# One core, attention and two MoE stages: a weight conversion's ScalarE and VectorE steps put into other slots of its schedule

## The chip, the core and the metric

The kernel runs on one core of a Trainium2 chip. The metric is the device time of one launch in microseconds (us). TensorE (PE, its weight loads apart as PEld), VectorE (DVE), ScalarE (ACT) and GpSimd (POOL) each take their instructions in the order in which the program wrote them; SyncE (SP) issues most loads, GpSimd's queue issues a few. An instruction that waits holds everything behind it on its own engine.

## What is computed

Three stages, all in fp32 accuracy. The second and the third are what matters here; the reference, cut down:

```
x = attention(q, k, v, alpha)                        # 3072 tokens x 384
for e in range(8):                                   # each token goes to one of 8 experts
    mask = argmax(x @ w_gate, axis=1) == e
    h = np.maximum(x[mask] @ w1[e], 0.0)             # 384 -> 1024
    out[mask] = gate_w * sigmoid(x @ w_output_gate)[e] * (h @ w2[e])   # 1024 -> 384
h = (out @ m_w1) * (out @ m_w2) @ m_w3               # the third stage's weights: float64
y = h @ m_w_out
```

The weights of the third stage come as 64-bit words. The kernel turns each word into an fp32 number itself, by integer steps on its two 32-bit halves.

## The kernel before, in words

Every matmul is done as three (`mm3`, lines 155 to 157): each operand is split into a rounded part and a rest, both of which TensorE takes at its fast rate. So every weight piece of 128 x 768 numbers costs ScalarE a copy (`w`, line 146) and VectorE a subtraction of two operands in SBUF (`w`, line 147); `feed` does that, some pieces ahead of their use.

The second stage runs expert by expert, in order of size (464 rows for the first, 360 for the eighth; `e` counts from 0). An expert has an **up** half and a **down** half of eight steps each, `f` = 0 to 7. A step is nine matmuls:

- up step `f`: nine matmuls `u<-xt,w`; then ScalarE writes the rounded `h` (line 822) and VectorE the rest (line 823), both out of the PSUM tile `u`. There are three `u` tiles, so up step `f` can't start before VectorE has done `h` of step `f-3`.
- down step `f`: nine matmuls `d<-h,w`. After `f` = 1, 3, 5 four (or three) transposes turn rows of the next expert, and ScalarE and VectorE write them as `xt` (lines 772, 773). The down half ends with three copies to `yT` on ScalarE (line 835).
- after each odd step there is one `feed`. After `f` = 5 of a down half GpSimd issues the gathers `xg` (line 754) of the expert after next.

Between the last two experts stand the 192 matmuls of `w_prime` (line 935 copies their result).

The conversion is a generator. The loop over experts calls `next(conv, None)` once after each up and each down step from expert 1 on: one such call is a **slot**. Each of the 23 pieces (`N_D`) takes four slots in turn, one piece after the other, and the last slot of each ends with the store of the result to `wm_d` in DRAM over GpSimd's queue (line 856). The stored pieces come back later as `raw` and are fed like the others. In the kernel before, slot 0 of a piece stands behind a step with `f` = 0 or 4. The steps of a piece: `Abs` of the high half into `cva` (ScalarE, line 121; two buffers), the low half scaled into `cvc` (ScalarE, line 122; one buffer), two one-operand steps on `cva` (VectorE, lines 124 and 125), one step with the high half and `cva` (VectorE, line 127), and the addition `cva + cvc` (GpSimd, line 130). `read()` issues the load of the piece after next into the buffer `mraw` that the piece has left (SP, line 852).

Of the kernel before, what the change touches and what calls it, by code (L numbers as in the profile page):

```python
# [11 lines left out]
U32 = mybir.dt.uint32  # L12
ACTF = mybir.ActivationFunctionType
ALU = mybir.AluOpType
# [38 lines left out]
def attention_then_moe_kernel(ctx, tc, pk0, pka, pkb, wbd_d, wexp, wmlp, cst_d, out):  # L53
    nc = tc.nc
    V, A, G, T, SP = nc.vector, nc.scalar, nc.gpsimd, nc.tensor, nc.sync
# [60 lines left out]
    def words(raw, read):  # L116
        w = raw.rearrange("p (n t) -> p n t", t=2)
        lw, hw = w[:, :, 0], w[:, :, 1]
        a, c = [pools["cv"].tile([128, NPC], I32, tag=t, name="cv" + t, bufs=n) for t, n in (("a", 2), ("c", 1))]
        af = a.bitcast(F32)  # L120
        A.activation(out=af, in_=hw.bitcast(F32), func=ACTF.Abs)  # L121
        A.activation(out=c, in_=lw.bitcast(U32), func=ACTF.Copy, scale=2.0 ** -29)
        yield
        V.tensor_scalar(out=af, in0=af, scalar1=TINY, scalar2=None, op0=ALU.max)
        V.tensor_scalar(out=a, in0=a, scalar1=3, scalar2=0x3FFFFFF8, op0=ALU.logical_shift_left, op1=ALU.bitwise_and)
        yield
        V.scalar_tensor_tensor(out=a, in0=hw, scalar=-(1 << 30), in1=a, op0=ALU.bitwise_and, op1=ALU.bitwise_or)
        read()
        yield
        G.tensor_tensor(out=a, in0=a, in1=c, op=ALU.add)  # L130
        return a.bitcast(F32)

# [349 lines left out]
    for j in range(NJ):  # L482
# [22 lines left out]
        if j == 5:  # L505
            A.activation(out=row, in_=cst[:, C_E4:C_E4 + E], func=ACTF.Copy, scale=1024.0)
            V.scalar_tensor_tensor(out=revc, in0=cst[:, C_E4:C_E4 + E], scalar=-1024.0 * E, in1=rev, op0=ALU.mult,
                                   op1=ALU.add)
# [7 lines left out]
        if j in R_RANK:  # L516
# [39 lines left out]
                           op0=ALU.mult, op1=ALU.add)  # L556
# [292 lines left out]
    def m_load(i):  # L849
        if i < N_D:  # L850
            mraw[i] = pools["mr"].tile([128, 2 * NPC], I32, tag="mr", name="mraw")
            SP.dma_start(out=mraw[i], in_=wmlp_w[i])

    def m_convert(i):
        a = yield from words(mraw.pop(i), lambda: m_load(i + 2))
        G.dma_start(out=wm_d[i], in_=a)
        yield
# [94 lines left out]
    def convert_all():  # L952
        m_load(0)
        m_load(1)
        for _ in range(4):
            yield
        for i in range(N_D):
            yield from m_convert(i)

    for e in range(E):  # L960
        if e == 1:
            for _ in conv:
                pass
            lr.close()
            pools["cv"] = cv2.enter_context(tc.tile_pool(name="cvb", bufs=1, reuse_waits="tile"))
            pools["mr"] = cv2.enter_context(tc.tile_pool(name="mr", bufs=2, reuse_waits="tile"))
            conv = convert_all()
# [168 lines left out]
```

## Time and profile before

| | |
|---|---|
| median of 3 runs | 732.04 us (731.51 to 733.71) |
| the profiled execution | 734.38 us, of which the span from first to last instruction is 732.6 |
| TensorE busy | 689.3 us, 94% of the span |
| VectorE, ScalarE, GpSimd busy | 400.3, 338.0, 208.4 us |
| granted TensorE clock | 0.98 over the span |
| stretch in which the pieces are converted, about 190 to 365 us | TensorE busy 173.51 of the 180 us from 185 to 365, VectorE 139.74, ScalarE 111.32, GpSimd 76.04 |

Attention ends at about 143 us. Experts 0 to 6 take 143 to 361 us, `w_prime` 361 to 395, expert 7 395 to 420, and the third stage the rest. Matmuls overlap, so one matmul's duration is longer than the distance to the next start; where the rest of this text speaks of a step's length it takes distances between starts.

### The profile page before, as it was taken

The page shows a single profiled execution, that of the slowest core. Times are in us where ns is not written, and L with a number is a line of the kernel's source. Part 1 is how long each engine was busy: PE and PEld are TensorE (multiplying, and loading weights), DVE is VectorE, ACT ScalarE, POOL GpSimd, SP SyncE. Part 2 cuts the span into 40 slices and gives each one's busy share as a digit, 9 for nine tenths or more (in the row PEclk, how much of TensorE's full clock was granted, in tenths as well). Part 3 has the DMA queues.
Part 4 walks back from the last instruction along what each step waited for, and adds up shares of the span by engine and source line. Part 5 has one row for each costly group of instructions (what it writes and reads, how often), then busy time and mean ns, then how long its engine had stood idle before and what let it go on. Part 6 is the DMA issues. An engine that isn't in the chain of part 4 may idle for free.

```text
span 732.6 us, 14570 instructions
## 1 busy us (share of the span) xinstructions
PE 689.3 (94%) x5856; PEld 610.3 (83%) x5856; DVE 400.3 (55%) x723; ACT 338.0 (46%) x666; POOL 208.4 (28%) x233
## 2 busy tenths in 40 slices
PE   6989998789999999998999999999999999999993
PEld 3877787378999998997999988988889889889893
DVE  6989897678689778687734565033132231340320
ACT  3787786344656756656634554133122222331320
POOL 2977685225153544435310000200101101002001
PEclk7999999899999999999999999999999999999997
DMA  8899883464686887878644500100000000001000
GB/s 275 234 256 252 247 261 109 139 214 162 221 296 234 303 285 262 299 250 297 216 150 152 173 1 0 44 1 12 32 1 22 21 1 34 11 1 44 0 12 33
DMA packets 28200, 101.73 MB, mean 139 GB/s; under 512 B 4784, under 2 KB 5208, under 8 KB 28128
## 3 DMA queue, kind: packets, MB, share of 16 engines
q1 hardware_dynamic: 21360, 77.26, 32.9%
q0 software_dynamic: 6624, 23.29, 9.2%
q8 instruction: 47, 0.77, 0.4%
q14 instruction: 25, 0.20, 0.1%
q10 hardware_dynamic: 144, 0.20, 0.1%
HBM read 82.25 MB, written 18.48 MB: 138 GB/s over the span
## 4 chain that ended last, share of the span: by engine, by line
PE 64%; DVE 4%; issue 4%; POOL 3%; ACT 2%; DMA 2%; POOLq 0%; ACTq 0%
PE pab L157 9%; PE pab L155 9%; PE pab L156 9%; PE o L157 4%; PE o L156 4%; PE o L155 4%; PE d L155 4%; PE u L155 4%; PE d L156 4%; PE d L157 4%; PE u L157 4%; PE u L156 4%; POOL cva L130 3%; DVE w L147 2%; ACT w L146 1%
## 5 line engine op out<-in xcount | busy, mean ns | idle before, releaser
L147 DVE TENSOR_TENSOR w<-raw,w 128x768 fp32r<-128x768 f32 x87 | 103.5, 1193 | 57.6 <-ACT w L146 56.3
L1029 DVE TENSOR_TENSOR p_s<-pab,a_s 128x512 f32<-128x512 f32 x48 | 33.2, 692 | 168.4 <-PE pab L157 168.4
L1043 POOL DMA_INDIRECT out_dram<-o_s,idx_o x24 | 23.4, 974 | 331.6 <-ACT o_s L1042 327.9
L155 PE MATMUL pab<-ys,w 128*128 128x512 f32 x288 | 113.8, 395 | 0.0
L157 PE MATMUL pab<-ys,w 128*128 128x512 f32 x288 | 113.8, 395 | 0.0
L156 PE MATMUL pab<-ys,w 128*128 128x512 f32 x288 | 113.8, 395 | 0.0
L146 ACT ACTIVATE w<-raw 128x768 fp32r<-128x768 f32 x87 | 73.0, 842 | 51.6 <-PE d L157 21.2
L1031 ACT ACTIVATE ab<-p_s 128x512 fp32r<-128x512 f32 x48 | 30.4, 634 | 105.5 <-DVE p_s L1029 105.5
L155 PE MATMUL u<-xt,w 128*128 128x464 f32 (+7 forms) x192 | 69.0, 360 | 8.8 <-DVE h L823 8.1
L130 POOL TENSOR_TENSOR cva<-cva,cvc 128x768 int32<-128x768 int32 x23 | 47.0, 2044 | 95.9 <-ACT cva L121 32.4
L156 PE MATMUL u<-xt,w 128*128 128x464 f32 (+7 forms) x192 | 67.6, 352 | 1.5 <-DVE xt L773 1.5
L155 PE MATMUL d<-h,w 128*128 128x464 f32 (+7 forms) x192 | 68.9, 359 | 0.0
L157 PE MATMUL u<-xt,w 128*128 128x464 f32 (+7 forms) x192 | 67.2, 350 | 0.0
L156 PE MATMUL d<-h,w 128*128 128x464 f32 (+7 forms) x192 | 66.9, 348 | 0.0
L157 PE MATMUL d<-h,w 128*128 128x464 f32 (+7 forms) x192 | 66.6, 347 | 0.0
L157 PEld LDWEIGHTS pab<-ys,w 128*128 128x128 f32 x288 | 54.0, 187 | 13.3
L156 PEld LDWEIGHTS pab<-ys,w 128*128 128x128 f32 x288 | 54.0, 187 | 12.9
L155 PEld LDWEIGHTS pab<-ys,w 128*128 128x128 f32 x288 | 54.0, 187 | 12.9
L155 PE MATMUL o<-wpp,ab 128*128 128x384 f32 x192 | 64.2, 334 | 0.0
L157 PE MATMUL o<-wpp,ab 128*128 128x384 f32 x192 | 64.2, 334 | 0.0
L156 PE MATMUL o<-wpp,ab 128*128 128x384 f32 x192 | 64.2, 334 | 0.0
L1032 DVE TENSOR_TENSOR ab<-p_s,ab 128x512 fp32r<-128x512 f32 x48 | 33.2, 693 | 33.6 <-ACT ab L1031 33.6
(187 smaller groups left out, 1436.1 us busy)
## 6 DMA issues: line engine op xcount, KB each, us to landing
raw<-in_wexp_dram SPq DMA_DIRECT2D x32, 768.0 KB, 5.1
mraw<-in_wmlp_dram SPq DMA_DIRECT2D x23, 768.0 KB, 4.3
pb<-in_pkb_dram SPq DMA_DIRECT2D x24, 384.0 KB, 5.0
wm_d<-cva POOLq DMA_DIRECT2D x23, 384.0 KB, 3.9
raw<-wm_d SPq DMA_DIRECT2D x23, 384.0 KB, 3.7
pa<-in_pka_dram SPq DMA_DIRECT2D x42, 192.0 KB, 4.9
x_d<-xs POOLq DMA_DIRECT2D x23, 192.0 KB, 4.6
pa<-in_pka_dram SPq DMA_DIRECT2D x42, 97.5 KB, 5.1
```

Source lines behind the costliest of these rows:

```text
L130: G.tensor_tensor(out=a, in0=a, in1=c, op=ALU.add)
L146: A.activation(out=hl[:, 0], in_=src, func=ACTF.Copy)
L147: V.tensor_tensor(out=hl[:, 1], in0=src, in1=hl[:, 0], op=ALU.subtract)
L155: T.matmul(out=ps, lhsT=sh, rhs=mh, start=start, stop=False)
L156: T.matmul(out=ps, lhsT=sh, rhs=ml, start=False, stop=False)
L157: T.matmul(out=ps, lhsT=sl, rhs=mh, start=False, stop=stop)
L1029: V.tensor_tensor(out=p_s, in0=pss[1], in1=a_s, op=ALU.mult)
L1031: A.activation(out=t[:, 0], in_=p_s, func=ACTF.Copy)
L1032: V.tensor_tensor(out=t[:, 1], in0=p_s, in1=t[:, 0], op=ALU.subtract)
L1043: G.indirect_dma_start(out=out[:, :], out_offset=bass.IndirectOffsetOnAxis(ap=idx_o[:, n:n + 1], axis=0), in_=o, in_offset=None)
```

## The change

The copy of the low half moves from slot 0 to slot 3, ahead of `read()` and the addition. VectorE's three steps, which stood in slots 1 and 2, stand together in slot 1; slot 2 is empty. The whole sequence starts one slot later, so slot 0 now stands behind `f` = 1 or 5.

```diff
         A.activation(out=af, in_=hw.bitcast(F32), func=ACTF.Abs)
-        A.activation(out=c, in_=lw.bitcast(U32), func=ACTF.Copy, scale=2.0 ** -29)
         yield
         V.tensor_scalar(out=af, in0=af, scalar1=TINY, scalar2=None, op0=ALU.max)
         V.tensor_scalar(out=a, in0=a, scalar1=3, scalar2=0x3FFFFFF8, op0=ALU.logical_shift_left, op1=ALU.bitwise_and)
-        yield
         V.scalar_tensor_tensor(out=a, in0=hw, scalar=-(1 << 30), in1=a, op0=ALU.bitwise_and, op1=ALU.bitwise_or)
+        yield
+        yield
+        A.activation(out=c, in_=lw.bitcast(U32), func=ACTF.Copy, scale=2.0 ** -29)
         read()
-        yield
         G.tensor_tensor(out=a, in0=a, in1=c, op=ALU.add)
...
-        for _ in range(4):
+        for _ in range(5):
             yield
```

ScalarE at the start of expert 6's up half, before (`h` is the rounded half of an up step, in order of `f`):

```order
L822 ACTIVATE h_5132<-u 128x376
L121 ACTIVATE cva<-mraw 128x768
L122 ACTIVATE cvc<-mraw 128x768
L822 ACTIVATE h_5149<-u 128x376
L146 ACTIVATE w_5152<-raw 128x768
L822 ACTIVATE h_5167<-u 128x376
L822 ACTIVATE h_5183<-u 128x376
L146 ACTIVATE w_5186<-raw 128x768
L822 ACTIVATE h_5204<-u 128x376
```

And with the change:

```order
L822 ACTIVATE h_5127<-u 128x376
L128 ACTIVATE cvc<-mraw 128x768
L822 ACTIVATE h_5145<-u 128x376
L146 ACTIVATE w_5148<-raw 128x768
L121 ACTIVATE cva<-mraw 128x768
L822 ACTIVATE h_5164<-u 128x376
L822 ACTIVATE h_5180<-u 128x376
L146 ACTIVATE w_5183<-raw 128x768
L822 ACTIVATE h_5199<-u 128x376
```

The copy `cvc` that now stands behind `h` of step 0 belongs to the piece whose `Abs` ran four slots earlier; the `Abs` of the next piece has moved one step down, behind `w`.

VectorE over the same steps, before:

```order
L823 SCALAR_TENSOR_TENSOR h_5132<-u,h_5132 128x376
L823 SCALAR_TENSOR_TENSOR h_5149<-u,h_5149 128x376
L147 TENSOR_TENSOR w_5152<-raw,w_5152 128x768
L124 TENSOR_SCALAR cva<-cva 128x768
L125 TENSOR_SCALAR cva<-cva 128x768
L823 SCALAR_TENSOR_TENSOR h_5167<-u,h_5167 128x376
L127 SCALAR_TENSOR_TENSOR cva<-mraw,cva 128x768
L823 SCALAR_TENSOR_TENSOR h_5183<-u,h_5183 128x376
L147 TENSOR_TENSOR w_5186<-raw,w_5186 128x768
```

And with the change:

```order
L823 SCALAR_TENSOR_TENSOR h_5127<-u,h_5127 128x376
L823 SCALAR_TENSOR_TENSOR h_5145<-u,h_5145 128x376
L147 TENSOR_TENSOR w_5148<-raw,w_5148 128x768
L823 SCALAR_TENSOR_TENSOR h_5164<-u,h_5164 128x376
L123 TENSOR_SCALAR cva<-cva 128x768
L124 TENSOR_SCALAR cva<-cva 128x768
L125 SCALAR_TENSOR_TENSOR cva<-mraw,cva 128x768
L823 SCALAR_TENSOR_TENSOR h_5180<-u,h_5180 128x376
L147 TENSOR_TENSOR w_5183<-raw,w_5183 128x768
```

`h` of step 2 now stands ahead of all three steps of the conversion instead of between them; `h` of step 3 stands behind all three, as before.

ScalarE at the start of expert 7, behind `w_prime`, one piece of the difference:

```order
+L822 ACTIVATE h0_5660<-u_5650 128x360
+L146 ACTIVATE w1_5663<-raw_5627 128x768
+L128 ACTIVATE cvc_5358<-mraw_5274 128x768
 L822 ACTIVATE h1_5679<-u_5669 128x360
-L146 ACTIVATE w1_5682<-raw_5650 128x768
+L146 ACTIVATE w1_5682<-raw_5627 128x768
 L822 ACTIVATE h2_5698<-u_5688 128x360
```

The last piece's copy, and with it its addition and store on GpSimd, now falls into the first slot of expert 7. GpSimd's own order is the same in both kernels.

## Rows read from the trace of the kernel before

**Rows 1.** TensorE's waits, 200 to 360 us: total, times, longest

```profile
PE u L155 <- DVE h L823: 5.1, 7, 0.9
PE u L156 <- DVE xt L773: 1.3, 1, 1.3
```

**Rows 2.** Timeline of TensorE, expert 6's up half: start, duration, [idle before]

```profile
331.56 0.34 PE L155 MATMUL u<-xt,w 128*128 128x376 f32 x1
...
332.59 0.33 PE L155 MATMUL u<-xt,w 128*128 128x376 f32 x1
334.25 0.44 PE L156 MATMUL u<-xt,w 128*128 128x376 f32 x1 [1.33 <-DVE xt L773]
334.52 0.33 PE L157 MATMUL u<-xt,w 128*128 128x376 f32 x1
...
342.25 0.44 PE L155 MATMUL u<-xt,w 128*128 128x376 f32 x1 [0.86 <-DVE h L823]
...
346.38 0.45 PE L155 MATMUL u<-xt,w 128*128 128x376 f32 x1 [0.78 <-DVE h L823]
...
348.04 0.34 PE L155 MATMUL d<-h,w 128*128 128x376 f32 x1
```

**Rows 3.** Timeline of VectorE in the same half

```profile
339.71 0.96 DVE L147 TENSOR_TENSOR w<-raw,w 128x768 fp32r<-128x768 f32 x1 [0.18 <-ACT w L146]
340.59 0.56 DVE L124 TENSOR_SCALAR cva<-cva 128x768 f32<-128x768 f32 x1
341.18 0.56 DVE L125 TENSOR_SCALAR cva<-cva 128x768 int32<-128x768 int32 x1
...
342.11 0.95 DVE L127 SCALAR_TENSOR_TENSOR cva<-mraw,cva 128x768 int32<-128x768 int32 x1
342.98 0.54 DVE L823 SCALAR_TENSOR_TENSOR h<-u,h 128x376 fp32r<-128x376 f32 x1
343.44 2.43 DVE L147 TENSOR_TENSOR w<-raw,w 128x768 fp32r<-128x768 f32 x1
345.79 1.15 DVE L823 SCALAR_TENSOR_TENSOR h<-u,h 128x376 fp32r<-128x376 f32 x2
```

**Rows 4.** Timeline of GpSimd: a gather and an addition

```profile
333.65 0.99 POOL L754 DMA_INDIRECT xg<-x_d,idx_c  x1 [0.30 <-issue]
...
343.21 1.84 POOL L130 TENSOR_TENSOR cva<-cva,cvc 128x768 int32<-128x768 int32 x1 [4.67 <-issue]
```

**Rows 5.** Timeline of ScalarE, end of expert 5 and expert 6's up half

```profile
329.88 0.90 ACT L122 ACTIVATE cvc<-mraw 128x768 int32<-128x768 uint32 x1 [3.15 <-POOL cva L130]
...
332.52 1.25 ACT L835 ACTIVATE yT<-d 128x388 f32 x3
...
344.25 0.90 ACT L121 ACTIVATE cva<-mraw 128x768 f32<-128x768 f32 x1 [2.33 <-DMA wm_d<-cva]
345.08 0.91 ACT L122 ACTIVATE cvc<-mraw 128x768 int32<-128x768 uint32 x1
345.90 0.46 ACT L822 ACTIVATE h<-u 128x376 fp32r<-128x376 f32 x1
346.26 0.83 ACT L146 ACTIVATE w<-raw 128x768 fp32r<-128x768 f32 x1
```

**Rows 6.** ScalarE's waits, 185 to 420 us: total, times, longest

```profile
ACT cvc L122 <- POOL cva L130: 28.7, 17, 3.1
```

**Rows 7.** The stores of the converted pieces (line 856), from issue to landing

```profile
DMA to landing us min/median/max: 3.0/3.9/6.6
```

**Rows 8.** Timeline of ScalarE and TensorE at the start of expert 7

```profile
396.41 0.47 ACT L822 ACTIVATE h<-u 128x360 fp32r<-128x360 f32 x1 [0.26 <-PE u L157]
399.03 0.84 ACT L146 ACTIVATE w<-raw 128x768 fp32r<-128x768 f32 x1 [2.15 <-DMA raw<-in_wexp_dram]
399.78 0.45 ACT L822 ACTIVATE h<-u 128x360 fp32r<-128x360 f32 x1
...
404.79 0.44 PE L155 MATMUL u<-xt,w 128*128 128x360 f32 x1 [0.21 <-DVE h L823]
```

More of the change, by code (lines that the diff above doesn't have):

```diff
@@ L125, in words @@
         V.tensor_scalar(out=a, in0=a, scalar1=3, scalar2=0x3FFFFFF8, op0=ALU.logical_shift_left, op1=ALU.bitwise_and)
+        V.scalar_tensor_tensor(out=a, in0=hw, scalar=-(1 << 30), in1=a, op0=ALU.bitwise_and, op1=ALU.bitwise_or)
         yield
-        V.scalar_tensor_tensor(out=a, in0=hw, scalar=-(1 << 30), in1=a, op0=ALU.bitwise_and, op1=ALU.bitwise_or)
+        yield
+        A.activation(out=c, in_=lw.bitcast(U32), func=ACTF.Copy, scale=2.0 ** -29)
         read()
-        yield
         G.tensor_tensor(out=a, in0=a, in1=c, op=ALU.add)
```

## The prediction

> **What bounds the kernel now.** TensorE is the bound: the page gives it 94% of the span, so only time in which it stands still, or is slow to start again, can be won. I read the waits of TensorE first, over the stretch in which pieces are converted. There it waits eight times: seven times in all 5.1 us for VectorE's `h`, and once 1.3 us for VectorE's `xt` [rows 1]. All eight lie in up halves, of experts 3 to 6. The timeline shows what a wait costs beside the gap [rows 2]: the matmul in front of the gap at 334.25 started at 332.59, so 1.66 us lie between two starts; a steady distance is 0.173 us (the six from 331.56 to 332.59 take 1.03), the gap is 1.33, and 0.16 are left. The next start comes 0.27 later instead of 0.17. A restart thus costs about 0.28 us more, and the eight waits 6.4 + 8 x 0.28 = 8.6 us. As a check, expert 6's half lasts from 331.56 to 348.04, 16.48 us, where 72 x 0.173 = 12.46 would do: 4.0 us lost, against 1.33 + 0.86 + 0.78 + 3 x 0.28 = 3.8 by the gaps. Small hitches make the rest, a factor of 1.06, so what can be won in the stretch is about **9.1 us**.
>
> Why `h` is late is read from VectorE and GpSimd side by side. GpSimd's addition runs from 343.21 to 345.05 [rows 4]. VectorE's subtraction `w`, which takes 0.96 us at 339.71, starts at 343.44 and takes 2.43: it ends at 345.87, 0.82 after the addition [rows 3]. It has been held until the addition was over. Behind it stands `h` of the next step, and TensorE waits until 346.38 [rows 2]. In the old order this collision is built in: the addition becomes free with VectorE's last step of the conversion, and the next but one on VectorE is the `w` of step 3.
>
> The Trainium skill ("SBUF — State Buffer", Who interferes with whom) states that a VectorE instruction with two SBUF inputs, or in a two-port mode, and a GpSimd instruction that reads SBUF exclude each other, and that the second to come is blocked for the whole of the first. These rows agree: 2.43 against 0.96 us.
>
> The second cause stands on ScalarE. `cvc` has one buffer, and its copy directly follows the addition of the piece before in time: ScalarE waits for that addition 17 times, 28.7 us in all [rows 6]. Such a wait of 3.15 us at 329.88 [rows 5] delays the third `xt`, and that is the 1.33 us of TensorE.
>
> **The change part by part.** *The copy three slots later.* It still follows the addition of the piece before, but that addition has then been free for some four steps (6.2 us), and itself takes 1.84. The 28.7 us of waits on ScalarE go, with the 1.33 us of TensorE. ScalarE's work is the same; it is spread over two steps instead of one.
>
> *VectorE's three steps in one slot, the addition behind the copy.* I go through expert 6's up half, the one with the shortest steps, from its first matmul at 0. From start to next start I take: on ScalarE `cvc` 0.82 and `Abs` 0.83, `h` 0.36 [rows 5], `w` 0.75 [rows 8]; on VectorE `w` 0.88, the first two steps 0.59 each, the third 0.87, `h` 0.46 [rows 3]; the addition 1.84. An up step is 9 x 0.173 = 1.56 us, and ScalarE's `h` comes about 0.2 behind it (idle of 0.26 at 396.41 [rows 8]).
> - ScalarE: the last `w` and the three `yT` (1.25 us in one row [rows 5]) hold it to 2.15; `h` of step 0 to 2.6, the copy from 2.5 to 3.4, `h` of step 1 to 3.8, `w` to 4.55, `Abs` to 5.35, `h` of step 2 to 5.75.
> - GpSimd: the addition from 3.55 to 5.4.
> - VectorE: `h` of step 1 to 4.35. `w` could start at 4.6 and is held to 5.4, 0.8 us instead of 1.5; it ends at 6.25, `h` of step 2 at 6.75. The three steps meet no addition, and end at 8.8. `h` of step 3 ends at 9.3; step 6 needs it at 6 x 1.56 = 9.36. `w`, then `h` of step 4 at 10.6; step 7 needs it at 10.92.
>
> So nothing waits, with 0.06 and 0.3 us to spare. The second addition of the half starts at about 10.2, when `w` leaves VectorE; what it holds is `w` of step 5, and no `h` behind that is needed before the down half is well under way. Experts 5, 4, 3 and 2 have steps of 1.61, 1.64, 1.69 and 1.76 us (rows of the expert against 376), so 0.3, 0.5, 0.8 and 1.0 us to spare. I take 9.1 us as won and put **0.3** against it, one restart in expert 6.
>
> *What is costed at nothing.* VectorE's work doesn't change; in the down halves it has only four `w`, three `xt` and two conversions to do, and `h` is long ready. The load of the piece after next is issued two slots later, and its `Abs` one, so it has five slots, some 8 us, instead of six; ScalarE's waits name no such load. On SP it now waits for ScalarE's copy instead of VectorE's third step, and the expert weights behind it are loaded two units ahead. The stores need a closer look, as the first rival.
>
> *One slot on.* The last piece's copy and addition now fall into expert 7's first slot, where ScalarE and VectorE have a `feed` in every step. The copy stands behind the `w` at 399.03 and so runs from 399.78 to 400.6 [rows 8]; the addition follows at 400.9, when VectorE's `w` ends, and holds the next `w` until 402.7. That `w` and `h` of step 2 end at 404.05, step 5 starts at 404.1, and step 6 after 1.49 us (1.56 x 360/376) at 405.6 instead of 404.79 [rows 8]: **0.8 us lost**. The bounds are 0, if later weight loads had held that stretch anyway, and 1.8, the addition's whole length. The store lands by 403.6 + 6.6 = 410.2 [rows 7], before its reload is issued behind step 7.
>
> **The sum.** -9.1 + 0.3 + 0.8 = -8.0 us. For the profiled execution that is 734.38 - 8.0 = 726.4. That one lies 2.3 us above the median of the runs, so the median should go from 732.04 to **724.0**.
>
> **The rivals.** *The stores come too late (slower).* With two buffers `cva`, an `Abs` needs the store of the piece two before it. Before, the addition ran right after slot 2; now it waits for the copy in slot 3, while `Abs` has moved by one slot only. The wait existed already: 2.33 us at 344.25 [rows 5]. In my walk down step 4 starts about 6.9 us ahead of the up half; the second `xt` and the copy keep ScalarE to -5.1, the addition runs to -3.1, and the store that frees the buffer of the `Abs` in step 1 is out at -2.3. It has to land by 4.45, in 6.7 us; the longest landing so far is 6.6, the median 3.9 [rows 7]. If landings stretched to L, the `Abs`, and with it the three steps and `h` of step 3, would be late by L - 6.7 in five experts. Less the 2.7 us to spare in all, with five restarts of 0.28, that costs 5 x (L - 6.7) - 1.3. At L = 8.6 the gain is gone (732); at 9.2 the time is **735.2**. Against it: the loads are spread out more evenly than before, so landings should not grow. I give 0.10 to the milder form, within 0.3% of before, and 0.08 to the one that is slower.
>
> *The addition runs into the three steps.* Where gathers keep GpSimd, the addition of step 0 starts late. A gather takes 0.99 us and 0.3 ahead of it [rows 4]; the four of experts 1 to 3 would end at about 3.2, in front of the addition at 3.55, so there is little to spare. If it started at 5.0 or later, it would hold the conversion on VectorE by up to 1.84 us; less what experts 2, 3 and 4 have to spare, with a restart each, that is 1.1 + 1.3 + 1.6 = 4.0 us, and the time **728.0**. I give it 0.14. By the same section of the Trainium skill's page "SBUF — State Buffer" this is what speaks against putting the three steps together: two of them are of the kind that has a two-port mode and the third has two SBUF inputs, so one late addition would hold all three.
>
> *As forecast*, 0.68, with its own range of 721.8 (both costs nothing, and hitches of a microsecond that the gaps don't count) to 726.5.
>
> **How the numbers follow.** A measurement of this kernel tells about 0.3%, 2.2 us, from no change. Faster holds the forecast and the late addition, 0.82; no change 0.10; slower 0.08. The range goes from 721.8 to 729.5, which leaves out the two forms of late stores and little else.
>
> **What would show it.** ScalarE's wait for the addition (line 122 before, 128 after) should be all but gone; TensorE's waits between 200 and 360 us should fall from 6.4 us to below 1; expert 6's up half should last 12.5 to 13 us; the `w` of step 3 should take 0.96 us and a `w` of step 1 or 5 up to 1.8; expert 7's up half should be longer by about 0.8. I am wrong if `Abs` waits for `wm_d` for more than 2 us in step 1, if the three steps on VectorE take over 2.1 us, or if TensorE waits as long for `h` of step 3 as it did for step 4.

## The result, and the profile after

The changed kernel takes 725.5 us at the median (723.37 to 728.94, seven runs) against 732.04 (730.92 to 734.06, seven runs): a ratio of 0.990, 95% interval 0.988 to 0.992. Forecast were 724.0 us with a range of 721.8 to 729.5. The profiled execution of the changed kernel took 726.71 us, with a span of 724.9.

TensorE's waits between 200 and 360 us, to be held against [rows 1]: total, times, longest.

```profile
PE u L155 <- DVE h L823: 2.0, 3, 1.0
```

Of 6.4 us 2.0 are left, and the wait for `xt` is gone. ScalarE's waits from 185 to 420 us on the conversion's tiles [rows 6]:

```profile
ACT cva L121 <- DMA wm_d<-cva: 9.6, 7, 2.8
...
ACT cva L121 <- DMA mraw<-in_wmlp_dram: 3.5, 5, 1.2
```

The 28.7 us in which the copy waited for the addition don't appear any more. What waits now is `Abs`, for the stores and for the loads of `mraw`; the second is new.

The three waits that TensorE has left all lie in expert 6's up half, as its timeline shows [rows 2]:

```profile
324.30 0.34 PE L155 MATMUL u<-xt,w 128*128 128x376 f32 x1
...
332.70 0.44 PE L155 MATMUL u<-xt,w 128*128 128x376 f32 x1 [0.31 <-DVE h L823]
...
335.22 0.44 PE L155 MATMUL u<-xt,w 128*128 128x376 f32 x1 [0.71 <-DVE h L823]
...
338.01 0.44 PE L155 MATMUL u<-xt,w 128*128 128x376 f32 x1 [0.98 <-DVE h L823]
...
339.65 0.34 PE L155 MATMUL d<-h,w 128*128 128x376 f32 x1
```

Taken from first matmul to first matmul in the timelines of the two kernels, the lengths are (us):

| | before | after | difference |
|---|---|---|---|
| up halves of experts 2, 3, 4, 5 | 14.11, 14.43, 14.88, 15.22 | 13.88, 13.41, 12.96, 12.80 | -5.6 |
| up half of expert 6 | 16.49 | 15.35 | -1.1 |
| expert 7, both halves | 25.07 | 25.76 | +0.7 |
| expert 1 to the third stage, all | 238.07 | 232.03 | -6.0 |

The down halves and `w_prime` (33.31 us in both) are as long as before. The spans differ by 7.7 us; the 1.6 us beyond the 6.0 lie ahead of expert 1, where the two kernels are the same: its first matmul stands at 181.73 us before and at 180.10 after. Over all the profiled executions of this document that point lies between 177.5 and 181.7 us, so the total of a single execution says less of the change than the stretch behind it.

### The profile page after: what moved, and what is told of

Same layout as the page of the kernel before. It is cut to its first block, busy times and chain, and to the rows that moved or that the text cites. A ratio compares the mean times of both kernels' runs of the same rounds, so it can differ in the third digit from the quotient of the medians.

```text
span 724.9 us, 14572 instructions
## 1 busy us (share of the span) xinstructions
PE 686.7 (95%) x5856; PEld 609.6 (84%) x5856; DVE 397.3 (55%) x723; ACT 339.1 (47%) x666; POOL 210.1 (29%) x233
## 4 chain that ended last, share of the span: by engine, by line
PE 69%; DVE 4%; DMA 3%; ACT 2%; issue 1%; POOLq 0%; ACTq 0%
PE pab L157 9%; PE pab L155 9%; PE pab L156 9%; PE d L155 5%; PE u L155 5%; PE o L157 4%; PE o L156 4%; PE o L155 4%; PE u L156 4%; PE u L157 4%; PE d L156 4%; PE d L157 4%; DVE w L147 2%; DMA wm_d<-cva 2%; PE x L759 1%
## 5 line engine op out<-in xcount | busy, mean ns | idle before, releaser
L147 DVE TENSOR_TENSOR w<-raw,w 128x768 fp32r<-128x768 f32 x87 | 97.4, 1125 | 51.0 <-ACT w L146 49.6
```

Of the source, the lines that this page charges most:

```text
L147: V.tensor_tensor(out=hl[:, 1], in0=src, in1=hl[:, 0], op=ALU.subtract)
```

## The experiments

All are compared with the kernel before in runs on the same chip; the ratio's 95% interval stands in brackets. "Lost" is how much longer the up halves of experts 2 to 6 took together, in the profiled execution, than the 65.4 us that they take at TensorE's steady pace (13.88, 13.41, 12.96, 12.80 and 12.37 us, the least of any version). It is 9.7 us in the kernel before and 3.0 in the changed one.

### The three parts of the change, one by one and in pairs

The change has three parts: the **late copy** (slot 3 instead of 0), the **three steps together** (slot 1), and the **shift** (five empty slots ahead instead of four). Late copy alone:

```diff
-        A.activation(out=c, in_=lw.bitcast(U32), func=ACTF.Copy, scale=2.0 ** -29)
         yield
...
-        read()
         yield
+        A.activation(out=c, in_=lw.bitcast(U32), func=ACTF.Copy, scale=2.0 ** -29)
+        read()
```

> Of the three parts of the change only the first: the low half's copy in slot 3, with VectorE's three steps still in two slots and no shift. Theory (two causes, ScalarE's wait for the addition and the hold of VectorE's w by the addition, and where the addition falls decides): ScalarE's wait for the addition is gone (28.7 us before, under 2), but the addition now starts behind step 3 and the steps of the conversion meet it there; up halves of experts 2 to 6 lose 4 to 7 us of their 9.7, time 727 to 729.5. Rival (the whole gain is ScalarE's wait): all of it comes with this part alone, the up halves lose 3 us or less and the time is 725.5 or less.

Three steps together alone (one `yield` moves from ahead of the third step to behind `read()`):

> Only the second part: VectorE's three steps in slot 1, the copy still in slot 0 with Abs, no shift. Theory: the addition is free one slot earlier, so the copy four slots on finds it done and ScalarE's wait goes here as well; the addition holds another w or the next conversion step; up halves of experts 2 to 6 lose 4 to 7 us of 9.7, time 727 to 729.5. Rival (putting the three steps together is what won): 725.5 or less, with w of step 3 free of the addition. Rival (three in one go delays h): no faster than 731.

Shift alone (`range(5)` in the kernel before):

> Only the third part: the kernel before, with the whole sequence one slot later. Theory: the addition and the copy collide as before, only under other steps; ScalarE waits 20 us or more for the addition, up halves of experts 2 to 6 lose 5 to 9 us, expert 7 0.5 more than before: 728 to 732. Rival (only the place relative to the steps counts): 725.5 or less.

The changed kernel without its shift (`range(4)`):

> The changed kernel without its shift: copy late and three steps together, but the sequence begins one slot earlier, and the last piece is done in expert 6 again. Theory: expert 7's up and down halves return to 25.1 us from 25.8, but the addition now starts behind step 3 and holds a w or h-carrying stretch there, so that experts 2 to 6 lose 4 to 6 us instead of 3.0: 726 to 728. Rival (the shift does nothing but cost the 0.7 us in expert 7): 724.8 or less.

The late copy with the shift, VectorE's steps still in two slots:

> The copy late and the shift, but VectorE's three steps still in two slots (1 and 2). Theory now: what the late copy cost without the shift (ScalarE waits 20 us and more for the load of mraw, which SP issues only behind the expert's weights) goes with the shift, since Abs then stands one step later while the weights' load keeps its place; and the addition starts behind the copy whether or not the three steps stand together. So it is as fast as the changed kernel: 0.988 to 0.993 of before, ScalarE's waits for mraw under 8 us. Rival (the three steps in one slot carry part of the gain): 0.994 or slower.

The three steps together with the shift, the copy early:

> VectorE's three steps together and the shift, but the copy in slot 0 with Abs. Theory: the addition starts as soon as the three steps are done, behind step 2, and holds w of step 3 as in the kernel before; ScalarE's copy has four slots less of distance than with the late copy, so its wait for the addition stays partly (10 us or more); up halves of experts 2 to 6 lose 3 to 6 us: 0.990 to 0.996 of before. Rival (the late copy adds nothing beside the other two): 0.990 or faster.

The changed kernel once more, in the runs of the last section below:

> The changed kernel once more, on the chip of the two others. Theory (the three steps in one slot are what makes expert 6 lose 3 us when Abs is late): 0.988 to 0.992 of before, slower than the version with the steps in two slots by 2 to 4 us, with 1 to 4 us lost in expert 6's up half. Rival (that difference was between chips): within 1.5 us of it.

Measured:

| late copy | together | shift | median us | ratio to before | lost |
|---|---|---|---|---|---|
| x | | | 733.38 | 1.001 [0.999, 1.003] | 9.0 |
| | x | | 727.83 | 0.993 [0.991, 0.995] | 5.1 |
| | | x | 728.07 | 0.994 [0.992, 0.996] | 5.5 |
| x | x | | 735.12 | 1.003 [1.001, 1.005] | 9.9 |
| x | | x | 722.50 | 0.986 [0.984, 0.988] | 0.0 |
| | x | x | 729.95 | 0.996 [0.995, 0.998] | 7.0 |
| x | x | x (again) | 726.51 | 0.992 [0.989, 0.994] | 3.7 |

Of the two kernels with a late copy and no shift the profiled execution was the fastest of twelve (728.88 and 732.12 us). Expert 1 starts at 177.5 and 179.2 us in them, which has nothing to do with the change; from there to the third stage they take 236.8 and 238.3 us, against 238.1 before. What the slower executions add was not traced.

The times of the three steps together and of the shift, each alone, came out as expected. The two together came out slower than expected, by a little in the time and with 7.0 us lost instead of 3 to 6. What was expected of ScalarE's wait for the addition was missed in all three: with the three steps together it was to go, and 15.6 us are left; with the shift it was to stay at 20 or more, and is 10.7; with both it was to stay at 10 or more, and this is left:

```profile
ACT cvc L122 <- POOL cva L130: 1.2, 3, 0.6
```

That last version parts the two ways in which the addition makes `h` late. ScalarE's wait is as good as gone, and TensorE still loses 7.0 us, for in each of the experts 2 to 6 the `w` of step 3 takes 2.37 to 2.42 us beside the addition, and the first matmul of step 7 comes 0.85 to 1.25 us late, 5.5 us in all. In expert 4, VectorE and TensorE:

```profile
280.19 2.41 DVE L147 TENSOR_TENSOR w<-raw,w 128x768 fp32r<-128x768 f32 x1
...
283.14 0.45 PE L155 MATMUL u<-xt,w 128*128 128x396 f32 x1 [0.92 <-DVE h L823]
```

The expectation for the late copy alone was missed: it wins nothing. So was that for the changed kernel without its shift. ScalarE's wait for the addition is gone in both, but two others take its place. ScalarE's waits from 185 to 420 us in the late copy alone:

```profile
ACT cva L121 <- DMA mraw<-in_wmlp_dram: 25.3, 9, 3.7
ACT cva L121 <- DMA wm_d<-cva: 14.7, 10, 3.0
```

In the timeline of SP's queue of the same kernel the load of `mraw` stands right behind that of the expert's weights, which waits for VectorE's `w` of step 3 or 7:

```profile
250.22 0.33 SPq L111 DMA_DIRECT2D raw<-in_wexp_dram  x1
250.66 0.38 SPq L852 DMA_DIRECT2D mraw<-in_wmlp_dram  x1
```

and on ScalarE's queue the `Abs` that wants it waits:

```profile
257.21 0.90 ACT L121 ACTIVATE cva<-mraw 128x768 f32<-128x768 f32 x1 [2.42 <-DMA mraw<-in_wmlp_dram]
```

With the shift `Abs` stands one step further behind that pair of loads, and the late copy has no wait for `mraw` at all; of its waits on `cva` this is left:

```profile
ACT cva L121 <- DMA wm_d<-cva: 7.0, 6, 2.3
```

So the shift, which the prediction took for a cost in expert 7, is what makes the late copy pay; without it the changed kernel is 0.3% slower than before. Putting the three steps together is worth 0.7% by itself, but with the other two it costs: late copy and shift without it are at 722.50 us, a ratio of 0.986 against 0.990 and 0.992 of the changed kernel's two comparisons. That is faster than was expected of it (0.988 to 0.993). Those were on other chips; the version with the last piece early, below, which is late copy and shift but for that one piece, ran beside the changed kernel on one chip: 722.29 against 726.51 us. In their traces expert 6's up half is 3.5 us shorter and expert 7, through that one piece, 1.1. The lost time, 0.0 against 3.0 and 3.7, says the same. So the rival by which the difference lies between chips falls.

### The addition left out

In the kernel before, the line of GpSimd's addition is taken out; the store then takes `cva` as VectorE leaves it.

```diff
-        G.tensor_tensor(out=a, in0=a, in1=c, op=ALU.add)
```

> The kernel before without GpSimd's addition: the store takes cva as VectorE leaves it, so the low bits of the third stage's weights are left out of the result. All else stays in its slot. Theory (the addition causes nearly all that the up halves lose, by holding VectorE's w and by making ScalarE's copy wait): ScalarE's wait for it is gone, every w takes 0.96 us, and the up halves of experts 2 to 6 lose under 2 us of 9.7: 0.985 to 0.990 of before. Rival (VectorE is simply full in the up halves, or Abs and copy back to back delay ScalarE): they still lose 4 us or more, 0.992 or slower.

722.22 us, a ratio of 0.986 [0.983, 0.988]; lost 0.3 us. The group of VectorE's `w` from 185 to 365 us of this kernel (busy, mean ns, idle before):

```profile
L146 DVE TENSOR_TENSOR w<-raw,w 128x768 fp32r<-128x768 f32 x52 | 49.7, 956 | 38.7 <-ACT w L145 37.8 <-PE u L156 0.2
```

And of the changed kernel:

```profile
L147 DVE TENSOR_TENSOR w<-raw,w 128x768 fp32r<-128x768 f32 x51 | 62.5, 1231 | 21.6 <-ACT w L146 20.8
```

Without the addition every `w` is at 0.96 us, and TensorE waits for nothing between 200 and 360 us. The addition was behind nearly all that the up halves lost. This doesn't part its two ways, the hold of `w` and ScalarE's wait, since both go with it. A third thing goes too: the store follows VectorE at once, and `Abs` waits for stores 1.4 us instead of 9.8.

### Abs without the store

The changed kernel with the result written into `cvc`, one buffer `cva` and two `cvc`, and `Abs` in VectorE's slot:

```diff
-        a, c = [pools["cv"].tile([128, NPC], I32, tag=t, name="cv" + t, bufs=n) for t, n in (("a", 2), ("c", 1))]
+        a, c = [pools["cv"].tile([128, NPC], I32, tag=t, name="cv" + t, bufs=n) for t, n in (("a", 1), ("c", 2))]
...
-        A.activation(out=af, in_=hw.bitcast(F32), func=ACTF.Abs)
         yield
+        A.activation(out=af, in_=hw.bitcast(F32), func=ACTF.Abs)
...
-        G.tensor_tensor(out=a, in0=a, in1=c, op=ALU.add)
+        G.tensor_tensor(out=c, in0=a, in1=c, op=ALU.add)
```

> The changed kernel with the addition's result written into cvc instead of cva, one buffer cva and two cvc (the same memory), and Abs in slot 1 right ahead of VectorE's three steps. The store then reads cvc, so Abs waits for no store any more, and cvc comes free eight slots later instead of five; the load of mraw has six slots. Theory (what expert 6 still loses, 3.0 us, is Abs waiting for the store of the piece two before): that wait (9.6 us in 7) is gone, expert 6's up half takes 12.4 to 13.0 us instead of 15.35, and the time is 0.984 to 0.988 of before. Rival (VectorE has no time to spare in expert 6, and h of step 3 behind the three steps is late anyway): expert 6 still loses 2 us or more, 0.989 or slower.

724.53 us, 0.988 [0.985, 0.990]; the wait of `Abs` for stores is gone, and expert 6's up half takes 12.41 us instead of 15.35. VectorE had the time: with the three steps still together nothing is lost once `Abs` comes when it is due. From expert 1 to the third stage the trace is 3.1 us shorter than the changed kernel's; the ratios of the two overlap and can't show it.

### The last piece out of expert 7

Once by starting the changed kernel's sequence four slots earlier (`range(1)`):

> The changed kernel with the whole sequence four slots earlier (it begins in the first step of expert 1 instead of the fifth), so that every step stands behind the same f as in the changed kernel and the last piece is done in expert 6. Theory: only expert 7 changes, whose halves take 25.1 us instead of 25.8, and expert 6, which then has no piece in its last four down steps: 0.5 to 1.0 us faster than the changed kernel, 0.987 to 0.990 of before. Rival (the last piece in expert 7 costs nothing that isn't lost anyway): no difference to the changed kernel's 0.990. Rival (the first loads aren't there so early and hold ScalarE in expert 1): slower than 0.991.

Expert 7 took 25.12 us instead of 25.76, as the theory has it. But the kernel is at 731.14 us, 0.998 [0.995, 1.000]: the second rival, larger than it was priced. Its timeline of ScalarE in expert 1 shows the first `Abs`:

```profile
184.17 0.84 ACT L146 ACTIVATE w<-raw 128x768 fp32r<-128x768 f32 x1
188.23 0.89 ACT L121 ACTIVATE cva<-mraw 128x768 f32<-128x768 f32 x1 [3.22 <-DMA mraw<-in_wmlp_dram]
```

The first `mraw` is not there yet, `h` stands behind the waiting `Abs`, and expert 1's up half loses 3.2 us. That does not make up the whole distance to the changed kernel's 725.5; its runs spread over 727.2 to 734.7 us, and what the longer ones add was not traced.

Then with the late copy and the shift, and the last piece's copy and addition one slot earlier:

```diff
...
         V.scalar_tensor_tensor(out=a, in0=hw, scalar=-(1 << 30), in1=a, op0=ALU.bitwise_and, op1=ALU.bitwise_or)
-        yield
+        if not last:
+            yield
         A.activation(out=c, in_=lw.bitcast(U32), func=ACTF.Copy, scale=2.0 ** -29)
...
```

> The copy late and the shift, VectorE's three steps in two slots, and for the last piece alone the copy and the addition one slot earlier, behind the last down step of expert 6. Theory: expert 7 gets back what the last piece cost there (its two halves 25.1 us instead of 25.7), everything else as with the late copy and the shift: 0.984 to 0.987 of before. Rival (the addition then disturbs the start of w_prime as much): its 33.3 us grow by 0.5 or more.

722.29 us, 0.987 [0.985, 0.990]. In the trace expert 7 takes 24.52 us instead of the 25.69 of late copy and shift, and `w_prime` keeps its 33.31. The microsecond is there in the trace; the times can't tell it from the 722.50 of that version.

## Why the prediction was right, point by point

**What TensorE waits for, and why.** Right. That `h` is late through the addition is shown by leaving it out: 9.7 us lost become 0.3. Both ways are real. The hold by itself costs 5.5 us where ScalarE hardly waits (three steps together and shift). In the trace of before 3.4 of the 9.7 us lie just ahead of step 7, behind the held `w` of step 3; the other 6.3 lie further ahead, most of them ahead of step 5 and in the wait for `xt`, where ScalarE's `h` or `xt` comes late behind its own wait. No version takes away the second way alone without bringing waits of its own, so these shares are read from a trace and not from a run.

**The 9.1 us to be won.** The pace gives 9.7 in the trace of before. Experts 2 to 5 won all that they had, 5.6 us, and in the way that the walk says: there the addition meets the `w` of step 1, which takes 1.30 to 1.47 us, and leaves that of step 3 alone. In expert 5, 4.7 and 9.1 us into the half:

```profile
302.40 1.47 DVE L147 TENSOR_TENSOR w<-raw,w 128x768 fp32r<-128x768 f32 x1 [0.17 <-ACT w L146]
...
306.82 0.95 DVE L147 TENSOR_TENSOR w<-raw,w 128x768 fp32r<-128x768 f32 x1
```

**The 0.3 us for expert 6.** This is the term that was off: it lost 3.0 us, and 3.7 in the second trace, that of the changed kernel run once more. The mechanism is the first rival's, in one expert where the rival reckoned with five, and the gathers of the second rival add to it in one of the two traces. In the walk `Abs` of step 1 starts at 4.45 us and finds its store landed. In the changed kernel's timelines, where the half starts at 324.30, ScalarE has

```profile
317.63 0.90 ACT L121 ACTIVATE cva<-mraw 128x768 f32<-128x768 f32 x1 [2.85 <-DMA wm_d<-cva]
...
330.78 0.91 ACT L121 ACTIVATE cva<-mraw 128x768 f32<-128x768 f32 x1 [1.92 <-DMA wm_d<-cva]
```

GpSimd

```profile
321.68 2.44 POOL L130 TENSOR_TENSOR cva<-cva,cvc 128x768 int32<-128x768 int32 x1 [5.54 <-DVE cva L125]
...
329.39 1.86 POOL L130 TENSOR_TENSOR cva<-cva,cvc 128x768 int32<-128x768 int32 x1
```

and VectorE

```profile
329.35 2.73 DVE L147 TENSOR_TENSOR w<-raw,w 128x768 fp32r<-128x768 f32 x1
332.10 0.55 DVE L823 SCALAR_TENSOR_TENSOR h<-u,h 128x376 fp32r<-128x376 f32 x1
332.56 0.55 DVE L123 TENSOR_SCALAR cva<-cva 128x768 f32<-128x768 f32 x1
333.15 0.56 DVE L124 TENSOR_SCALAR cva<-cva 128x768 int32<-128x768 int32 x1
333.74 0.96 DVE L125 SCALAR_TENSOR_TENSOR cva<-mraw,cva 128x768 int32<-128x768 int32 x1
334.62 0.55 DVE L823 SCALAR_TENSOR_TENSOR h<-u,h 128x376 fp32r<-128x376 f32 x1
```

An `Abs` in the down half has already waited 2.85 us for a store. So the addition of down step 4 starts at 321.68, 2.6 us ahead of the half instead of 4.9, and the three gathers behind it keep the next addition until 329.39, 5.1 us in. It holds `w` for 1.8 us, `Abs` waits another 1.9, and the three steps in one piece put `h` of step 3 to 335.17, 10.9 us in, where step 6 wanted it at 9.36. Here the held `w` and the late `Abs` make `h` of step 2 late by about the same time.

In the second trace the late `Abs` does it alone. The addition starts 4.0 us in, `w` ends at 330.27, and then VectorE stands still for `h` of step 2, which ScalarE writes behind `Abs`; ScalarE and VectorE there:

```profile
330.73 0.89 ACT L121 ACTIVATE cva<-mraw 128x768 f32<-128x768 f32 x1 [2.52 <-DMA wm_d<-cva]
...
332.02 0.55 DVE L823 SCALAR_TENSOR_TENSOR h<-u,h 128x376 fp32r<-128x376 f32 x1 [1.75 <-ACT h L822]
```

The store that it waits for took 7.8 us to land, where the prediction reckoned with 6.6 at most. So the prediction's first sign of being wrong, a wait of more than 2 us in step 1, was met in this trace and just missed in the first (1.92); TensorE's waits (2.0 us, not below 1) and the length of the half (15.35, not 12.5 to 13) missed what it said would show it.

Either remedy alone sets it right, the store out of `Abs`'s way or the three steps in two slots. With the first the walk holds to its end: `h` of step 3 is done 9.15 us in (9.3 in the walk) and step 6 starts at 9.27 (9.36). In the late copy with the shift, whose half starts at 322.37, the walk comes out nearly to the letter up to `h` of step 2:

```profile
326.18 0.55 DVE L823 SCALAR_TENSOR_TENSOR h<-u,h 128x376 fp32r<-128x376 f32 x1 [0.45 <-ACT h L822]
326.91 1.57 DVE L147 TENSOR_TENSOR w<-raw,w 128x768 fp32r<-128x768 f32 x1 [0.18 <-ACT w L146]
328.40 0.54 DVE L823 SCALAR_TENSOR_TENSOR h<-u,h 128x376 fp32r<-128x376 f32 x1
...
329.92 0.54 DVE L823 SCALAR_TENSOR_TENSOR h<-u,h 128x376 fp32r<-128x376 f32 x1
```

The addition beside them:

```profile
325.81 1.85 POOL L130 TENSOR_TENSOR cva<-cva,cvc 128x768 int32<-128x768 int32 x1 [0.54 <-ACT cvc L128]
```

`w` ends 6.1 us in (6.25 in the walk) and `h` of step 2 at 6.6 (6.75); `h` of step 3, with only two steps ahead of it, at 8.1 instead of 9.3. The addition, 3.4 us in (3.55), holds `w` and not the `h` that runs beside it in 0.55 us. The Trainium skill ("SBUF — State Buffer", Who interferes with whom) states that a VectorE instruction with at most one SBUF input, outside the two-port modes, does not contend with GpSimd; `h` has one input in PSUM, and these rows agree.

**What was costed at nothing.** The load of `mraw` with five slots instead of six was nearly a mistake. It costs 3.5 us of ScalarE's waits in the changed kernel, which TensorE hardly sees, but 25.3 and 22.3 us in the two kernels with a late copy and no shift. The prediction looked at the slots between issue and use and had the expert's weights behind this load on SP; in the changed kernel they stand right ahead of it. The step that it counted as a pure cost was what kept this away, and that the forecast held in spite of it was luck.

**The 0.8 us in expert 7.** 0.7 measured, and by the mechanism told: the copy comes behind the first `w`, the addition behind the copy, and the next `w`, which took 0.95 us in the kernel before, is held. GpSimd and VectorE:

```profile
392.30 1.81 POOL L130 TENSOR_TENSOR cva<-cva,cvc 128x768 int32<-128x768 int32 x1 [40.39 <-ACT cvc L128]
...
393.33 1.61 DVE L147 TENSOR_TENSOR w<-raw,w 128x768 fp32r<-128x768 f32 x1 [0.20 <-ACT w L146]
```

Moving the last piece out of expert 7 gives 0.6 back in one version and 1.2 in another.

**The sum.** -5.6 - 1.1 + 0.7 = -6.0 us in the two traces, -6.5 between the medians, against -8.0. In the prediction's terms that is -9.7 + 3.0 + 0.7: the 2.7 us too little for expert 6 are what the range had to take up.

## What to carry to other kernels

Where one engine's instruction can hold another's, and that other one feeds the engine that bounds the kernel, look not only at how much such work there is but at which instruction it meets: here the same addition cost 9.7 us or nothing, by when it ran. A step that is moved takes its loads with it; look at what stands ahead of each on its queue, not at how many slots lie between. And parts of a reordering don't add up: of the three here one alone won nothing, two won 0.6 to 0.7% each, the best pair 1.4% and the worst lost 0.3%, so each is worth a run with and without the others.

## What was not expected of the hardware

The store of a converted piece, the same 384 KB on the same queue, took longer to land once the order had changed (line 856, minimum, median and maximum) [rows 7]:

```profile
DMA to landing us min/median/max: 3.1/5.8/7.9
```

The prediction had argued that landings should not grow, since the loads would be spread out more evenly. They were drawn together: the load of `mraw` was issued 2.8 us ahead of one of the expert's weights, and now follows one after 0.4. SP's queue in the kernel before, then in the changed one:

```profile
252.12 0.33 SPq L852 DMA_DIRECT2D mraw<-in_wmlp_dram  x1
254.88 0.34 SPq L111 DMA_DIRECT2D raw<-in_wexp_dram  x1
```

```profile
251.02 0.33 SPq L111 DMA_DIRECT2D raw<-in_wexp_dram  x1
251.46 0.37 SPq L852 DMA_DIRECT2D mraw<-in_wmlp_dram  x1
```

Between 200 and 352 us the 768 KB loads of `mraw` had a median of 6.6 us to landing in the changed kernel and 4.3 in the kernel before; those of the expert's weights, as large, went the other way, from 6.2 to 5.0. The mean share of the DMA engines from 185 to 365 us hardly moved (0.78 before, 0.80 after). So the order of issues changed, and hardly the sum of bytes. In the nine profiled executions in which the load of `mraw` follows within a microsecond, at the median, it has 6.6 to 7.0 us; in the other four, where 5 us or more lie between, 4.3 to 5.0. What lengthened the stores no run here separates.
